# Attention chained into a gated feed-forward layer on one core: the first two batches' softmax, loads and products regrouped, the last output tile cut in two unequal pieces

## The chip, the cores and the metric

The kernel runs on one core of a Trainium2 chip. The time is what the device takes for one execution, in microseconds (us); runs of the same program differ by about 0.1%. Five engines work side by side, each through its own list of instructions in a fixed order: TensorE (PE in the profile; its weight loads have a row of their own, PEld), VectorE (DVE), ScalarE (ACT), GpSimd (POOL) and SyncE (SP). An instruction waits on semaphores, and whatever stands behind it on its engine waits too. Transfers are issued from the lists of POOL, SP and ACT and land later.

## The reference

For 8 batches, 8 heads, 576 tokens and a head size of 64, 32 packed queries per head attend to the keys and values; the tokens then attend to the 32 packed rows. The result, 4608 tokens by 512, goes through a feed-forward layer of 512 by 2048 and 2048 by 512.

```python
def sm_attn(qq, kk, vv):
    s = scale * np.matmul(qq, kk.transpose(0, 1, 3, 2))
    s = s - np.max(s, axis=-1, keepdims=True)
    a = np.exp(s)
    a = a / (np.sum(a, axis=-1, keepdims=True) + 1e-09)
    return np.matmul(a, vv)
p_packed = sm_attn(p, k, v)
out = sm_attn(q, p_packed, p_packed)
...
h = x @ w_in
g = np.where(pos, h, np.where(neg, 0.0, (h + beta) ** 2 / (4.0 * beta)))
return (g @ w_out).astype(np.float32)
```

With beta = 1, pos is h >= 1 and neg is h <= -1.

## The kernel before, in words

All products are in bf16. Each batch goes through these steps, named as in the code.

- **trans** (line 369) turns keys and queries by 12 TensorE transposes per four heads, followed by a copy out of PSUM (`kT`, `qT`). From batch 3 on the transpose is a DMA issued by SP (`turned`, line 511).
- **scores** (387): packed queries times keys, then Exp on ACT (`ex`).
- **packed** (405): `ex` times values, and the sums of `ex` by a matmul with ones (`pk`); the two halves of the tokens are added into `ppT`, and `rs` takes reciprocals of the sums. Batch 0 does this by halves of the heads (g = 0, 1), the other batches at once.
- **weights** (444): for each g, `s2` (tokens' queries times `ppT`), Exp to `eT` on ACT, `sm` (the sums of `eT` by a matmul with blocks of ones), Ln, then Exp of minus that (`rc`) on ACT, and `A` = `eT` times `rs` times `rc` on DVE.
- **mk** (485): `M` = packed rows times `w_in`, in four pieces f of 512 columns, each copied out of PSUM by ACT or DVE. The attention's second product and the layer's first are so folded into one.
- **hidden_tile** (542), 16 per batch: `h` = M times A, four matmuls of 288 columns; on ACT Prelu (`x`, first); second, an add and max on DVE or a Relu on ACT; third, on DVE, min and multiply into `hT`. Tile fi needs piece fi // 4 of M and both g of A.
- **out_tile** (585): per pair of batches nine tiles of 128 tokens, each the sum of 16 steps, matmuls of 512 columns over `hT` and `w_out`. Tiles 0 to 3 of a pair need the first batch alone, tile 4 both. The first pair's tiles 0 to 3 are cut after step 12 (`cuts`): the sum so far is copied to `part` and added at the end. A finished tile is copied to `ob` and stored in rows of 512 floats from SP. The very last tile is computed as two halves of 256 columns, copied by ACT and DVE at once and stored from their two queues (`done_last`).

The order of all this is made when the program is built: every step is a `Task` with a cost per engine from the table `C`, a key and its dependencies, and `Plan.run` (109) puts the tasks, by estimated times, into the engines' lists. A step that may go to either of ACT and DVE (`both`) goes where it is expected to end first. The order on the chip is then fixed; `C` decides order and engine, not durations. PSUM has three double slots (`W`), which all products but the output tiles share, and two slots for output tiles (`O`); five buffers hold `x`. While fewer than three output slots have been taken, the planner fills TensorE's expected waits with matmuls on zeros (`FILL`).

Loads go from POOL's list in the order of the lines 291 to 312: batch 0 in halves of four heads, in the order `FIRST` (k, v, q, k, v, q); then pieces of `w_in` and `w_out` in turns; then batch 1's k (two halves), v (one load), q (two halves), the last piece of `w_out` and the rest of p.

Of the kernel before, what the change touches and what calls it, by code (L numbers as in the profile page):

```python
# [11 lines left out]
C = dict(load=3.5666, half=1.46, w_in=2.57, w_out=2.57, rest=1.25, out=9, p=4.05, land=2.0125, xt=6.5, xland=11, tpp=0.06, tp=0.042, sc=0.034, pk=0.9765, s2=0.2862, sm=0.245, M=0.2415, h=0.49, o=0.217, switch=0.05, join=0.1604, pTc=0.1, Tca=1.12, Tcd=0.76, ex=0.82, ppT=0.42, ppo=0.41, ppa=0.4, ppd=0.2, rs=0.18, eT=0.74, ln=0.65, rc=0.68, A=0.82, Mca=1, Mcd=1.22, x=0.65, ta=0.683, td=0.489, hT=0.758, oba=0.585, obd=0.6276, array=0.2, wake=1.2, warm=4.2, early=0.3, tell=0.034, feed=0.085, slack=0.51, margin=0.1717, wait=0.5)  # L12
NW, NO, NX, NB = 3, 2, 5, 6
DW, FILL = 256, 512
TURNED = 3
# [166 lines left out]
def kernel(  # L182
# [108 lines left out]
    FIRST = [("k", 0), ("v", 0), ("q", 0), ("k", 1), ("v", 1), ("q", 1)]  # L291
# [9 lines left out]
    add_weights("in", 0)  # L301
    add_weights("in", 1)
    add_weights("out", 0)
    add_weights("in", 2)
    add_weights("out", 1)
    add_weights("in", 3)
    add_weights("out", 2)
    add_load("k", 1, 2)
    add_load("v", 1, 1)
    add_load("q", 1, 2)  # L310
    add_weights("out", 3)
# [46 lines left out]
    def attention(b, key):  # L358
# [9 lines left out]
        def trans(nm, i, dst, prev):  # L368
# [11 lines left out]
            t = add(PE, C["tp"] * 12, ky, [L[nm, b, i]] + prev, mm, takes="W", readers=1, mode=0)  # L380

            def cp(eng):
                w = 4 * E * TP
                copy(dst()[:, i, :w].rearrange("p (j c) -> p j c", j=X), box["tp"][:, :, :w // 2])(eng)
            return t, [both(cp, C["Tca"], C["Tcd"], ky, [t], frees=t)]
# [58 lines left out]
        def weights(g, deps, r):  # L444
# [10 lines left out]
            def exp2(eng):  # L455
                box["eT"] = att.tile([P, X, HALF], bf16, tag="eT", name="eT")
                nc.scalar.activation(box["eT"], box["s2"][:, :, :HALF], AF.Exp, scale=rs()[:, g, 1:])  # L457

            def mm2():
                sm = box["sm"] = wide([P, X, FW], f32, "sm")  # L460
                for x in range(X):
                    nc.tensor.matmul(sm[:, x, :HALF], onesblk, box["eT"][:, x], start=True, stop=True)  # L462

            def ln(eng):
                box["ln"] = att.tile([P, X, HALF], f32, tag="ln", name="ln", bufs=1)
                nc.scalar.activation(box["ln"], box["sm"][:, :, :HALF], AF.Ln)  # L466

            def inv(eng):
                box["rc"] = att.tile([P, X, HALF], f32, tag="rc", name="rc")
                nc.scalar.activation(box["rc"], box["ln"], AF.Exp, scale=-1.0)  # L470

            def norm(eng):
                nc.vector.scalar_tensor_tensor(A()[:, g], box["eT"], rs()[:, g, :1], box["rc"], ALU.mult, ALU.mult)  # L473
            p_ = K.get((b - 1, "A" + str(g)), [])
            t, j = yield ky, C["s2"], deps + p_, mm
            e_ = add(ACT, C["eT"], ky, [t, r] + p_, exp2, frees=(t, j))
            t2 = add(PE, C["sm"], km, [e_], mm2, takes="W", readers=1, mode=0)
            l_ = add(ACT, C["ln"], km, [t2] + last.get("ln", []), ln, frees=t2)
            i_ = add(ACT, C["rc"], km, [l_] + p_, inv)
            a_ = add(DVE, C["A"], km, [i_] + K.get((b - 2, "h"), []), norm)  # L480
            last["ln"] = [i_]
            K[b, "A" + str(g)] = [a_]
            yield t, e_, a_

        def mk(f, deps):
# [13 lines left out]
            if (b, f) == (0, 0):  # L499
                yield t, add(DVE, C["Mcd"], ky, [t], cp, frees=(t, j))  # L500
# [206 lines left out]
```

## Time and profile before

| what | us |
|---|---|
| median of 3 runs | 250.54 (250.51 to 250.75) |
| the profiled execution's own time | 249.87 |
| its span, from the first to the last instruction | 247.8 |
| PE busy within the span | 237.5 (96%) |
| DVE busy | 180.7 (73%) |
| ACT busy | 186.2 (75%) |

The profiled execution took 0.67 us less than the median of the runs, and 2.07 us of it lie outside the span. Matmuls are pipelined, so that their busy times overlap; in the rows of the timeline the distance of two starts says more than a duration. In rows of groups the columns are line, engine, operation, tiles, shapes and count, then busy us and mean ns of one, then the engine's idle time before them and who ended it. A window's row has the busy time of PE, PEld, DVE, ACT and POOL, the granted clock of TensorE, the DMA engines' share and GB/s.

### The profile page before, as it was taken

What the parts mean: (1) busy time and instruction counts of PE and PEld (TensorE: products, weight loads), DVE (VectorE), ACT (ScalarE), POOL (GpSimd) and SP (SyncE); (2) the same over time, 40 slices, a digit from 0 to 9 for tenths busy, and PEclk for the clock granted to TensorE, in tenths of its full rate; (3) what the DMA queues carried; (4) which work ended last, traced back from release to release, by engine and by line L of the source; (5) the groups of instructions that cost most, each with busy time, mean ns of one, the idle gap of its engine ahead of it and who ended that gap; (6) DMA issues with size and microseconds to landing.
All of it is one profiled execution on the core that took longest, in us unless ns stands there. A gap on an engine that the chain in (4) does not pass through costs nothing.

```text
span 247.8 us, 5398 instructions
## 1 busy us (share of the span) xinstructions
PE 237.5 (96%) x2191; PEld 137.5 (55%) x2191; DVE 180.7 (73%) x312; ACT 186.2 (75%) x294; POOL 29.3 (12%) x44
## 2 busy tenths in 40 slices
PE   7879899999989999999999999999999999999993
PEld 2545466467636744665456644665466546654452
DVE  5455998889997987798859884799579967992000
ACT  3358895899889998698769888698888886982110
POOL 8632331212001030011001100000000000000000
PEclk9999999999999999999999999999999999999998
DMA  6999999999999999879998984641571121112223
GB/s 100 201 207 207 206 203 196 203 221 257 167 191 154 237 205 222 193 108 171 151 171 141 163 166 93 138 93 38 95 93 42 33 54 44 45 42 85 56 74 85
DMA packets 54825, 34.37 MB, mean 139 GB/s; under 512 B 27536, under 2 KB 50320, under 8 KB 54800
## 3 DMA queue, kind: packets, MB, share of 16 engines
q0 software_dynamic: 24672, 18.55, 50.0%
q1 hardware_dynamic: 29968, 15.34, 31.9%
q8 instruction: 17, 0.28, 0.5%
q10 hardware_dynamic: 160, 0.13, 0.2%
q14 instruction: 8, 0.07, 0.1%
HBM read 37.22 MB, written 9.44 MB: 188 GB/s over the span
## 4 chain that ended last, share of the span: by engine, by line
PE 79%; DMA 10%; DVE 6%; ACT 2%; issue 1%; POOL 1%; ACTq 0%; POOLq 0%
PE o L601 47%; PE h L549 21%; DMA w_in_sb<-in_moe_w_in_dram 8%; PE mp L494 3%; DVE hT L564 3%; DMA k<-in_k_dram 3%; PE pk L418 2%; PE sp L398 2%; PE tp L377 2%; PE sm L462 1%; DVE x L559 1%; PE s L452 1%; PE pk L424 1%; DVE pT L320 1%; ACT rc L470 1%
## 5 line engine op out<-in xcount | busy, mean ns | idle before, releaser
L601 PE MATMUL o<-w_out_sb,hT 128*128 128x512 bf16 (+1 forms) x592 | 144.5, 374 | 0.7 <-DVE hT L564 0.6
L564 DVE SCALAR_TENSOR_TENSOR hT<-x 128x576 bf16<-128x576 f32 x128 | 94.5, 755 | 5.4 <-ACT x L561 2.6
L554 ACT ACTIVATE x<-h 128x576 f32<-128x576 f32 x128 | 77.8, 656 | 12.6 <-PE h L549 9.9
L601 PEld LDWEIGHTS <-hT 128*128 128x128 bf16 x592 | 55.8, 98 | 55.7 <-issue 5.8
L549 PE MATMUL h<-A,M 128*128 128x288 bf16 x512 | 75.1, 286 | 0.5 <-ACT M L320 0.5
L549 PEld LDWEIGHTS <-M 128*128 128x128 bf16 x512 | 49.5, 98 | 21.5 <-issue 1.1
L559 DVE TENSOR_SCALAR x<-x 128x576 f32<-128x576 f32 x87 | 39.9, 458 | 11.0 <-ACT x L554 11.0
L561 ACT ACTIVATE x<-x 128x576 f32<-128x576 f32 x41 | 27.2, 683 | 0.1
L320 ACT COPY ob<-o 128x512 f32<-128x512 f32 (+1 forms) x19 | 10.9, 575 | 19.4 <-PE o L601 19.3
L320 DVE COPY ob<-o 128x512 f32<-128x512 f32 (+1 forms) x14 | 9.4, 668 | 22.0 <-PE o L601 22.0
L320 ACT CAST M<-mp 128x1024 bf16<-128x1024 f32 x22 | 21.3, 1019 | 3.2 <-PE mp L494 3.2
L473 DVE SCALAR_TENSOR_TENSOR A<-eT,rs,rc 128x576 bf16<-128x576 bf16 x16 | 13.0, 814 | 6.1 <-ACT rc L470 6.1
L320 DVE CAST M<-mp 128x1024 bf16<-128x1024 f32 x10 | 12.1, 1220 | 6.4 <-PE mp L494 6.4
L401 ACT ACTIVATE ex<-sp 96x768 bf16<-96x768 f32 x16 | 13.0, 813 | 4.4 <-PE sp L398 4.3
L457 ACT ACTIVATE eT<-s,rs 128x576 bf16<-128x576 f32 x16 | 11.3, 740 | 4.7 <-PE s L452 4.7
L466 ACT ACTIVATE ln<-sm 128x576 f32<-128x576 f32 x16 | 10.4, 651 | 3.8 <-PE sm L462 3.4
L260 POOL DMA_DIRECT2D q<-in_q_dram x10 | 7.4, 744 | 47.6 <-DMA qT<-q 33.3
L494 PE MATMUL mp<-w_in_sb,ppT 64*32 64x512 bf16 x256 | 10.5, 380 | 2.3 <-DMA w_in_sb<-in_moe_w_in_dram 2.2
L260 POOL DMA_DIRECT2D k<-in_k_dram x10 | 7.5, 753 | 44.1 <-DMA kT<-k 27.5
L676 PE MATMUL o<-zeros 128*128 128x512 bf16 (+1 forms) x39 | 10.8, 406 | 1.2 <-DVE zeros L248 1.2
L470 ACT ACTIVATE rc<-ln 128x576 f32<-128x576 f32 x16 | 10.9, 683 | 0.5
L398 PEld LDWEIGHTS <-kT 128*128 128x128 bf16 x192 | 7.6, 98 | 2.8 <-DVE kT L320 1.0
(50 smaller groups left out, 117.2 us busy)
## 6 DMA issues: line engine op xcount, KB each, us to landing
out_dram<-ob SPq DMA_DIRECT2D x23, 192.0 KB, 2.8
v<-in_v_dram POOLq DMA_DIRECT2D x7, 576.0 KB, 18.3
k<-in_k_dram POOLq DMA_DIRECT2D x6, 576.0 KB, 12.4
q<-in_q_dram POOLq DMA_DIRECT2D x6, 576.0 KB, 12.1
out_dram<-ob SPq DMA_DIRECT2D x24, 128.0 KB, 2.9
w_in_sb<-in_moe_w_in_dram POOLq DMA_DIRECT2D x4, 512.0 KB, 14.6
w_out_sb<-in_moe_w_out_dram POOLq DMA_DIRECT2D x4, 512.0 KB, 16.9
out_dram<-ob SPq DMA_DIRECT2D x23, 64.0 KB, 2.0
```

The costliest lines, as they stand in the source:

```text
L260: nc.gpsimd.dma_start(tok[nm, b][:, hs].rearrange("p h c d -> p h (c d)"), SRC[nm][b, hs].rearrange("h (p c) d -> p h (c d)", c=NC))
L320: return lambda eng: nc.vector.tensor_copy(out_, in_) if eng == DVE else nc.scalar.copy(out_, in_)
L401: nc.scalar.activation(ex()[:, :, i].rearrange("p e x a n -> p e (x a n)"), box["sp"], AF.Exp, scale=scale)
L470: nc.scalar.activation(box["rc"], box["ln"], AF.Exp, scale=-1.0)
L473: nc.vector.scalar_tensor_tensor(A()[:, g], box["eT"], rs()[:, g, :1], box["rc"], ALU.mult, ALU.mult)
L494: nc.tensor.matmul(mp[a * NP:(a + 1) * NP, g], pp_of(y, h), w_in_sb[y * D:(y + 1) * D, h // 2, f * FW:(f + 1) * FW], start=True, stop=True)
L549: nc.tensor.matmul(h[:, hf, :HALF], T[b, "M"][:, g, fi * P:(fi + 1) * P], T[b, "A"][:, g, hf], start=(g == 0), stop=(g == G - 1))
L554: nc.scalar.activation(box["x"], box["h"][:, :, :HALF], AF.Prelu, bias=-1.0, alpha=0.5)
L559: nc.vector.tensor_scalar(x, x, 1.0, 0.0, ALU.add, ALU.max)
L561: nc.scalar.activation(x, x, AF.Relu, bias=1.0)
L564: nc.vector.scalar_tensor_tensor(hT[:, fi, col:col + S].rearrange("p (a t) -> p a t", a=2), box["x"], 1.0, box["x"], ALU.min, ALU.mult)
L601: nc.tensor.matmul(o, hT[:, fi, i * P:(i + 1) * P], w_out_sb[:, fi, cs], start=(fi == 0 or fi in cuts), stop=(fi + 1 in cuts))
```

## The change

- The table `C` has new estimates, three new entries (`klo`, `khi`, `part`), and the keys of batch 0 and of the later batches are in another order.
- Loads: batch 0 comes as k0 k1 v0 q0 v1 q1. What follows is `ORDER`: three pieces of `w_in` and two of `w_out`, then batch 1's first half of k, of v and second half of k, the last piece of `w_in`, and so on; batch 1's v comes in halves too, and its `packed` step goes by halves of the heads.
- Batch 0: the copies of turned keys and queries are two instructions each; the softmax of g = 1 (`eT`, `sm`, `ln`, `rc`, `A`) goes by halves of the tokens, 288 columns each; every piece of M waits for the sums `sm` of g = 1; the first piece of M is copied in two halves, by g. M's pieces 1 to 3 wait for hidden tiles 0, 4 and 8.
- The first pair: two tiles instead of four are cut, after 8 steps instead of 12.
- The last batch: `A` is written in another order of the tokens, by two instructions per g, and rows are stored by that order.
- The last tile: two pieces of 384 and 128 columns, one after the other on TensorE; the first is copied by DVE and stored from SP, the second copied and stored by ACT.

```diff
+PARTS, CUT = 2, 8
+ORDER = "i0 i1 i2 o0 o1 k0 v0 k1 i3 v1 o2 q0 q1 o3"
...
-    FIRST = [("k", 0), ("v", 0), ("q", 0), ("k", 1), ("v", 1), ("q", 1)]
+    FIRST = [(nm[0], int(nm[1])) for nm in "k0 k1 v0 q0 v1 q1".split()]
...
+            parts = [slice(j, j + 1) for j in range(X)] if b == 0 else [slice(X)]
...
-            return t, [both(cp, C["Tca"], C["Tcd"], ky, [t], frees=t)]
+            part = 0.55 if len(parts) > 1 else 1.0
+            return t, [both(lambda eng, js=js: cp(eng, js), C["Tca"] * part, C["Tcd"] * part, ky, [t], frees=t) for js in parts]
...
+            parts = [slice(x, x + 1) for x in range(X)] if (b, g) == (0, 1) else [slice(X)]
...
+            def norm(eng, xs):
+                if b == B - 1:
+
+                    for x in range(X):
+                        o, e, r_ = [v.rearrange(w, e=E) for v, w in ((A()[:, g, x], "p (t e) -> p t e"),
+                                    (box["eT"][:, x], "p (e t) -> p t e"), (box["rc"][:, x], "p (e t) -> p t e"))]
+                        nc.vector.scalar_tensor_tensor(o, e, rs()[:, g, :1], r_, ALU.mult, ALU.mult)
+                    return
...
+            first_sm = K[b, "sm1"] if b == 0 else []
+            n = G if (b, f) == (0, 0) else 1
+            t, j = yield ky, C["M"], deps + [L["in", f]] + K.get((b - 2, "h"), []) + first_sm, mm, n
...
-        pk, pc, r = zip(*([packed((0,), [e0]), packed((1,), [e1])] if b == 0 else [packed((0, 1), [e0, e1])] * G))
+        pk, pc, r = zip(*([packed((0,), [e0]), packed((1,), [e1])] if b == 0 or b == 1 and "v0" in ORDER else [packed((0, 1), [e0, e1])] * G))
...
-        cuts = [12, KF] if pr == 0 and i < 4 else [KF]
+        cuts = [CUT, KF] if pr == 0 and i < PARTS else [KF]
+        pieces = [slice(0, 3 * d_model // 4), slice(3 * d_model // 4, d_model)] if end else [slice(0, d_model)]
...
+            elif end:
+                add(ACT if j else DVE, C["oba"] if j else C["obd"], b_key(pr, i), prev, fn,
+                    frees=owner, takes="ob", holds=C["out"])
...
-    names = "kT0 sc0 pk0 qT0 s20 kT1 sc1 pk1 sm0 qT1 s21 M0 sm1 M1 M2 M3".split()
+    names = "sc0 kT0 qT0 kT1 sc1 pk0 s20 pk1 sm0 s21 sm1 M0 M1 qT1 M2 M3".split()
...
+            for f in range(1, NF):
+                K[b, "M"][f].deps.append(K[b, "h"][4 * f - 4])
```

188 lines of the change are left out of this document (106 added, 82 removed).

## The prediction

> **What bounds the kernel now.** On the page TensorE is busy nearly throughout, so I read the busy times by stretch first, and then the timeline of the stretches where it is not full.
>
> ```profile
> 0.00:20.64 20.64, 16.43 (x185) 8.39 (x186) 10.16 (x26) 9.02 (x15) 12.14 (x22) 1.00 1.10 173
> 20.64:49.06 28.42, 27.09 (x300) 16.05 (x298) 24.75 (x41) 23.31 (x37) 7.82 (x10) 1.00 1.33 203
> 49.06:72.95 23.89, 23.09 (x243) 14.55 (x242) 21.92 (x40) 22.92 (x34) 2.32 (x3) 1.00 1.28 210
> 72.95:218.40 145.45, 145.45 (x1333) 85.59 (x1333) 117.81 (x198) 122.63 (x197) 7.01 (x9) 1.00 0.72 123
> 218.40:243.90 25.50, 25.46 (x135) 12.91 (x132) 5.64 (x10) 8.04 (x15) 0.00 (x0) 1.00 0.29 73
> 243.90:247.80 3.90, 0.00 (x0) 0.00 (x0) 0.42 (x1) 0.26 (x1) 0.00 (x0) 0.83 0.23 67
> ```
>
> From 72.95 us on TensorE is busy 145.45 of 145.45 us: nothing is to be won there, only lost. The change can win in three places: the 20.64 us before the first hidden tile (mostly matmuls on zeros and waits), the 1.33 + 0.80 us that TensorE stands idle up to 72.95, where VectorE and ScalarE are busy over 90% of the third stretch, and the 3.9 us after the last matmul.
>
> ```profile
> 1.20 2.96 PE L676 MATMUL o<-zeros 128*128 128x512 bf16 x7 [1.20 <-DVE zeros L248]
> 4.46 2.00 PE L676 MATMUL o<-zeros 128*128 128x512 bf16 x9
> 10.64 0.68 PE L377 MATMUL tp<-ident,k 96*128 96x96 bf16 x12 [0.17 <-DMA k<-in_k_dram]
> 13.54 0.68 PE L377 MATMUL tp<-ident,q 96*128 96x96 bf16 x12 [0.59 <-DMA q<-in_q_dram]
> 15.41 0.49 PE L452 MATMUL s<-qT,ppT 64*32 64x288 bf16 x8
> 17.02 0.41 PE L494 MATMUL mp<-w_in_sb,ppT 64*32 64x512 bf16 x8 [1.12 <-DMA w_in_sb<-in_moe_w_in_dram]
> 17.81 0.41 PE L462 MATMUL sm<-eT,onesblk 128*128 128x288 bf16 x2
> 19.54 0.41 PE L494 MATMUL mp<-w_in_sb,ppT 64*32 64x512 bf16 x8 [0.46 <-DMA w_in_sb<-in_moe_w_in_dram]
> 20.64 3.13 PE L549 MATMUL h<-A,M 128*128 128x288 bf16 x24
> 29.70 0.41 PE L494 MATMUL mp<-w_in_sb,ppT 64*32 64x512 bf16 x8 [0.60 <-DMA w_in_sb<-in_moe_w_in_dram]
> ```
> ```profile
> 14.26 0.76 DVE L320 COPY qT<-tp 128x1152 bf16<-128x1152 bf16 x1 [2.14 <-PE tp L377]
> 17.51 1.22 DVE L320 CAST M<-mp 128x1024 bf16<-128x1024 f32 x1 [1.05 <-PE mp L494]
> 18.31 0.65 ACT L466 ACTIVATE ln<-sm 128x576 f32<-128x576 f32 x1 [1.60 <-PE sm L462]
> 19.00 0.68 ACT L470 ACTIVATE rc<-ln 128x576 f32<-128x576 f32 x1
> 19.71 0.82 DVE L473 SCALAR_TENSOR_TENSOR A<-eT,rs,rc 128x576 bf16<-128x576 bf16 x1 [0.98 <-ACT rc L470]
> 21.33 3.91 ACT L554 ACTIVATE x<-h 128x576 f32<-128x576 f32 x7 [0.31 <-PE h L549]
> ```
>
> Read the chain to 20.64: the last q half lands at 13.5; transposes, copy, s at 15.41; then the sums sm stand in TensorE's list behind M's first piece, which waits for its weights until 17.02, so sm starts at 17.81 though ScalarE had long ended eT; ln, rc and A follow, and A ends at 20.53. Landings are paced: a half of 288 KB per (13.54 - 10.64) / 2 = 1.45 us, a piece of weights per (29.70 - 19.54) / 4 = 2.54 us (four lie between those waits).
>
> **The change, part by part**, by the order that the changed planner writes.
>
> *Head.* Loads: the six halves end at 13.5 as before; the first weights at 17.0 and 19.5; then by 2.54 and 1.45: third w_in 22.1, w_out 24.6 and 27.2, batch 1's k 28.6, v 30.1, k 31.5, the last w_in 34.1 (29.7 before), v 35.5, w_out 38.1, q 39.5 and 41.0. Copy of q in two halves, both on VectorE: ends about 15.1, as before. Sums now stand ahead of M: eT by halves 15.5 to 16.4, sm 16.0 and 16.4, then ln, ln, rc, rc. A half costs by two ScalarE copies below (512 columns 0.586, 256 columns 0.372) the same fixed 0.16 and half the rest, so 0.41 and 0.44 for ln and rc: rc ends 17.45 and 17.8. VectorE's half of M's copy, 17.5 to 18.15, stands ahead of the two A: these end at 18.6 and 19.05. ScalarE's half of M is ready at 18.45. TensorE has M at 17.02, then seven zeros matmuls (0.216 each, as an output step below) until 18.87: hidden tile 0 starts at 18.9, all 1.7 us earlier, of which M's second piece, now behind it, takes back 0.34.
>
> [...]
>
> *18.9 to 49: new waits.*
>
> ```profile
> L564 DVE SCALAR_TENSOR_TENSOR hT<-x 128x576 bf16<-128x576 f32 x128 | 94.5, 755 | 5.4 <-ACT x L561 2.6
> L559 DVE TENSOR_SCALAR x<-x 128x576 f32<-128x576 f32 x87 | 39.9, 458 | 11.0 <-ACT x L554 11.0
> L561 ACT ACTIVATE x<-x 128x576 f32<-128x576 f32 x41 | 27.2, 683 | 0.1
> L320 ACT CAST M<-mp 128x1024 bf16<-128x1024 f32 x22 | 21.3, 1019 | 3.2 <-PE mp L494 3.2
> L320 ACT COPY ob<-o 128x512 f32<-128x512 f32 x18 | 10.5, 586 | 16.6 <-PE o L601 16.5
> L320 DVE COPY ob<-o 128x512 f32<-128x512 f32 x13 | 8.9, 687 | 3.2 <-PE o L601 3.2
> L320 DVE COPY kT<-tp 128x1152 bf16<-128x1152 bf16 x2 | 1.5, 758 | 1.3 <-PE tp L377 1.3
> L320 DVE COPY pT<-tpp 64x768 bf16<-64x768 bf16 x3 | 1.6, 549 | 0.9 <-ACT pT L320 0.9
> 218.56 25.31 PE o L601 x133
> 156.36 1.96 PE h L549 x16
> ```
>
> A hidden tile takes TensorE 0.49 us (1.96 / 4), an output step 0.216 (25.31 over 101 steps and 32 of half width). M's second piece follows hidden tiles 0 to 2, and its copy (1.02, ScalarE) stands behind three x and one Relu: x starts 0.69 after its tile (20.64 to 21.33) and the next 0.56 later, so x at 19.6, 20.1, 20.6, Relu 21.3 to 22.0, copy until 22.85. Tile 4 needs it: TensorE, done with tile 3 at 21.2, fills 5.5 zeros matmuls and goes on at 22.95: 1.75 lost (0.55 less if the copy were never late, 1.0 more if it slipped by one copy). Tiles 4 to 7 and M's third piece then run to 25.4, eight output steps to 27.15, just when the second w_out lands (27.2); tile 8; then batch 1's keys, due at 28.6, hold TensorE for 0.55 (up to 1.45 more if the transfers are one half later, nothing if earlier). From there I find some 0.15 us of small waits up to the end of M: each later load (31.5, 34.1, 35.5, 38.1, 39.5, 41.0) lands before TensorE asks for it, and the last four hidden tiles follow M's last piece from about 37. Lost in all 2.45, against 1.33 idle before (and shorter waits, which overlapping busy times hide).
>
> Batch 1's hidden tiles then start at 50.7 rather than 49.06, but TensorE has by then done five output steps (1.08) and two sets of key transposes of batch 2 (1.04) that came later before: as if at 48.6, ahead by 0.45. By the single terms it is 1.7 - 0.34 - 2.45 + 1.33 = 0.24 and the waits that the busy times hide.
>
> *50 to 73.*
>
> ```profile
> 49.06 0.65 PE L549 MATMUL h<-A,M 128*128 128x288 bf16 x4 [0.47 <-ACT M L320]
> 72.73 0.39 PE L601 MATMUL o<-w_out_sb,hT 128*128 128x512 bf16 x1 [0.56 <-DVE hT L564]
> 64.48 0.76 DVE L564 SCALAR_TENSOR_TENSOR hT<-x 128x576 bf16<-128x576 f32 x1
> 65.65 0.76 DVE L564 SCALAR_TENSOR_TENSOR hT<-x 128x576 bf16<-128x576 f32 x1
> ```
>
> Before, this stretch ends on VectorE, at 1.17 us per tile (64.48 to 65.65). Between batch 1's last A and its last hT VectorE's list loses one part copy and one addition (0.69 each), one add-and-max (0.46), two pT copies (1.1) and the copy of p (0.43), and gains a copy each of kT and qT (0.76 each): 1.85 less. I walk its last hT to 70.8 instead of 72.67, and TensorE through tiles 4 and 5 with 0.3 us of waits, instead of 0.80 idle and some shorter ones: finished at 71.45 instead of 72.95. Both then stand at the same place, M's pieces of batch 2: ahead by 1.5 us.
>
> *73 to 218.* Matmuls the same. M's pieces 1 to 3 move behind the softmax sums, and the sums stand 14 or more output steps (3.0 us) ahead of the first hidden tile, which ln, rc and A (0.65 + 0.68 + 0.82) fit into. In the last batch A as four strided halves (0.5 each, perhaps 0.3 more) lies beside 22 output steps and three pieces of M. Cost: 0; below nothing is impossible, since TensorE is full, and above see the rivals.
>
> *Tail.*
>
> ```profile
> 243.78 0.37 ACT L320 COPY ob<-o 128x256 f32<-128x256 f32 x1 [2.80 <-PE o L601]
> 243.89 0.42 DVE L320 COPY ob<-o 128x256 f32<-128x256 f32 x1 [18.80 <-PE o L601]
> 244.34 0.79 SPq L622 DMA_DIRECT2D out_dram<-ob  x2
> DMA to landing us min/median/max: 1.9/2.1/2.4
> ```
>
> Matmul columns are the same. Before: DVE's copy to 244.31, two transfers issued one after the other, the second 0.37 later, landed 2.1 later at 246.8; the span ends 1.0 after. Now 128 columns are left when the matmuls end: a ScalarE copy of 0.27 (the step from 512 to 256 columns carried on) from 243.89, one transfer at 244.2, landed 246.1 to 246.3. The 384 columns are copied 0.9 earlier (0.56) and land by 246.0. Won 0.6 (0.4 to 0.7).
>
> *Sum:* 1.5 + 0.6 = 2.1; I take 2.0, since a walk leaves out small waits. The profiled execution took 249.87 with a span of 247.8; so span 245.8, execution 247.9, and against the median, which stands 0.67 higher, 250.54 - 2.0 = 248.5.
>
> **The rivals.**
>
> 1. *The early start runs dry.* If M's second copy or batch 1's keys come later by the upper ends above, or the last w_in, 4.4 us later than before, holds tiles 12 to 15 and with them VectorE, the 1.5 is eaten and the tail stays: 250.54 - 0.6 = 249.9. For it speaks that every load and every VectorE gap counts here; against it that output tiles 2 and 3 give TensorE work in between, and that VectorE's list is shorter.
> 2. *Slower: the clock.* The rows at 1.20 and 4.46 show zeros matmuls at 0.42 and then at 0.22 each: TensorE runs at half rate until some 3 us of dense matmuls have passed. The change issues 5.5 instead of 6.5 of them first and only 1.5 before 7 us, none between p's transposes (4.5) and the keys (6.3). If half rate stays, the filler before tile 0 lasts twice 1.51 and M another 0.34, 1.85 later, and hidden tiles for some 3 us at half rate lose 1.5 more: 248.5 + 3.35 = 251.9. It decides for slower once more than 2 us are lost so.
> 3. *Slower: a wait per batch in the full stretch*, as the 0.47 at 49.06, because M's pieces now come just ahead of the hidden tiles: 6 x 0.47 = 2.8, so 251.3. With 0.33 each nothing is left of the gain (250.5).
>
> [...]
>
> **How the numbers follow.** My walk: 0.60, with its own range 247.5 to 249.4 (the bounds of the waits). Rival 1: 0.18, 249.4 to 250.4, half of it below 250.0. Rival 2: 0.08; rival 3: 0.10, a third of it within 0.5 of no change. More gained than walked: 0.04. About 0.2% (0.5 us) is what a measurement can tell. Faster 0.60 + 0.04 + 0.09 = 0.73; same 0.09 + 0.03 = 0.12; slower 0.15. The range 247.4 to 250.8 leaves the slower cases out.
>
> **What would show it.** The first hidden tile at 18.9, its sums sm at 16 to 16.6, before M's first piece at 17.0; TensorE waiting before hidden tile 4 on ScalarE's M and before batch 1's keys on the DMA; tiles 4 and 5 done near 71.5; the last landing some 0.6 earlier after the last matmul. Wrong it would be by zeros matmuls at 0.42 after 5 us, by hidden tiles held past 51 us, or by idle TensorE after 73.

## The result, and the profile after

The changed kernel takes 250.69 us (median of 22 runs, 249.89 to 252.03), the kernel before, measured beside it, 250.06 (22 runs, 249.72 to 251.28: runs of one program differ by 0.6% here, not by the 0.1% of the first three). The ratio is 1.0032, 95% interval 1.002 to 1.0045: slower by 0.6 us, near the upper end of the range (250.8) and on the other side of no change, where I had forecast 2.0 less. The changed kernel's times fall into two groups, 15 runs from 249.89 to 250.84 and 7 from 251.59 to 252.03; the profiled run (252.03, span 250.22) is of the second. The kernel before's profiled run took 249.87, 0.19 below its median.

The stretches of the changed kernel, cut at the same events as before: the first hidden tile, batch 1's first hidden tile, the end of output tile 5, the last matmul. The columns are length, then busy time (and instructions) of PE, PEld, DVE, ACT and POOL, the granted clock, DMA share and GB/s.

```profile
0.00:21.68 21.68, 17.00 (x159) 10.12 (x162) 9.31 (x30) 10.48 (x19) 11.95 (x22) 1.00 1.10 173
21.68:54.05 32.37, 30.41 (x337) 18.56 (x342) 27.14 (x46) 27.09 (x42) 9.56 (x12) 1.00 1.33 203
54.05:75.40 21.35, 20.46 (x212) 13.14 (x214) 19.10 (x34) 20.47 (x33) 1.55 (x2) 1.00 1.28 210
75.40:246.90 171.50, 169.22 (x1440) 97.75 (x1464) 124.38 (x206) 130.05 (x212) 7.09 (x9) 1.00 0.74 113
246.90:250.22 3.32, 0.04 (x1) 0.00 (x0) 0.00 (x0) 0.27 (x1) 0.00 (x0) 0.97 0.24 79
```

In the fourth row TensorE was not idle for the 2.28 us that the row leaves: 24 matmuls have no record there (1440, against 1464 weight loads). In e1 of the experiments, which differs by nine matmuls on zeros at the start and has all records there, it is busy 171.35 of 171.45 us.

Five output steps and two sets of key transposes (2.12 us of TensorE) stand ahead of batch 1's first hidden tile now and behind it before, as the prediction says; the table sets them off. It gives for each stretch its length minus that of the kernel before, in us. The last column is the kernel e8 of the experiments, the changed kernel with its clock, its copies and its last store mended.

| stretch | predicted | after | e8 |
|---|---|---|---|
| to the first hidden tile | -1.74 | +1.04 | -1.00 |
| to batch 1's first hidden tile | +1.26 | +1.83 | +1.65 |
| to the end of tile 5 | -1.02 | -0.42 | -0.45 |
| to the last matmul | 0 | +0.55 | +0.50 |
| to the end | -0.60 | -0.58 | -0.59 |
| sum | -2.10 | +2.42 | +0.11 |

(For example, second row, after: 32.37 - 2.12 - 28.42 = 1.83.) The tail came as predicted. The rest did not.

The table sets single traces side by side, and the kernel before's is one of its shorter executions. By it e8 comes out 0.11 longer, while by medians e8 is 0.56 shorter than the kernel before. How far traces of one program differ, e3 and e15 show (both are the kernel before with the new tail alone): their second stretch takes 28.42 and 29.18 us. M's last weights land at 29.62 and 30.36, and only in the second does TensorE wait for them long. First e3, then e15:

```profile
29.66 0.41 PE L501 MATMUL mp<-w_in_sb,ppT 64*32 64x512 bf16 x8 [0.38 <-ACT x L561]
```
```profile
30.41 0.41 PE L501 MATMUL mp<-w_in_sb,ppT 64*32 64x512 bf16 x8 [1.39 <-DMA w_in_sb<-in_moe_w_in_dram]
```

Their last matmuls start at 243.65 and 244.31. A difference below some 0.7 us between the ends of two traces therefore shows nothing by itself; which wait stands where is read from them all the same.

The head, from the timeline of the changed kernel:

```profile
1.19 2.53 PE L728 MATMUL o<-zeros 128*128 128x512 bf16 x6 [1.19 <-DVE zeros L256]
6.87 0.84 PE L728 MATMUL o<-zeros 128*128 128x512 bf16 x2
...
12.61 0.46 DVE L326 COPY qT<-tp 128x576 bf16<-128x576 bf16 x1 [0.76 <-PE tp L383]
...
13.10 0.64 ACT L326 COPY qT<-tp 128x576 bf16<-128x576 bf16 x1 [0.65 <-DVE qT L326]
...
15.49 1.16 PE L383 MATMUL tp<-ident,q 96*128 96x96 bf16 x12
...
16.45 1.48 PE L728 MATMUL o<-zeros 128*128 128x512 bf16 x3
...
18.82 0.28 PE L477 MATMUL sm<-eT,onesblk 128*128 128x288 bf16 x1 [0.20 <-ACT eT L471]
...
19.61 0.28 PE L477 MATMUL sm<-eT,onesblk 128*128 128x288 bf16 x1 [0.50 <-ACT ln L482]
19.82 0.41 PE L529 MATMUL mp<-w_in_sb,ppT 64*32 64x512 bf16 x8
...
20.16 1.69 PE L728 MATMUL o<-zeros 128*128 128x512 bf16 x7
...
21.68 1.63 PE L589 MATMUL h<-A,M 128*128 128x288 bf16 x12
```

Three things are to be seen. Matmuls on zeros start 0.42 us apart up to those at 16.45 and 0.22 from 20.16 on, and twelve transposes take 1.16 instead of 0.68: TensorE runs at half rate until 17.94, where the granted clock is first recorded (before: 4.14). The second half of a copy, on ScalarE, starts when VectorE's first half ends, and names it as what it waited for. And the second half of the sums waits for the Ln of the first. The sums do stand ahead of M's first piece, as predicted, but at 18.82 and 19.61 instead of 16.0 and 16.4.

Around batch 1's first hidden tile, and the tail:

```profile
51.02 1.59 ACT L326 COPY pT<-tpp 64x768 bf16<-64x768 bf16 x2
...
52.64 0.56 DVE L326 COPY pT<-tpp 64x768 bf16<-64x768 bf16 x1 [1.14 <-ACT pT L326]
53.23 0.76 DVE L326 COPY kT<-tp 128x1152 bf16<-128x1152 bf16 x1
53.24 0.79 ACT L326 COPY pT<-tpp 64x768 bf16<-64x768 bf16 x1 [0.63 <-DVE pT L326]
...
54.05 1.83 PE L589 MATMUL h<-A,M 128*128 128x288 bf16 x12 [0.93 <-DVE kT L326]
...
246.14 0.56 DVE L326 COPY ob<-o 128x384 f32<-128x384 f32 x1 [24.71 <-PE o L647]
...
247.02 0.27 ACT L326 COPY ob<-o 128x128 f32<-128x128 f32 x1 [2.91 <-PE o L647]
247.31 0.37 ACTq L662 DMA_DIRECT2D out_dram<-ob  x1
```

The pT copies of batches 2 to 7 alternate between ScalarE and VectorE, one after the other, and with them VectorE's copy of kT, which holds the slot that the hidden tile waits for. My walk had no wait there. The row gives it as 0.93; counted from where the last output step would have let TensorE go on (nine of them, 0.216 apart, from 51.01) it is 1.09, since a matmul's recorded time reaches some 0.16 beyond the start of the next. Waits of TensorE below are counted in this second way unless a row is named. The last copy takes the 0.27 forecast.

### The profile page after: what moved, and what is told of

The parts are those of the page before. It is cut to its first block, busy times and chain, and to the rows that moved or that the text cites. A ratio compares the mean times of both kernels' runs of the same rounds, so it can differ in the third digit from the quotient of the medians.

```text
span 250.2 us, 5377 instructions
## 1 busy us (share of the span) xinstructions
PE 237.1 (95%) x2145; PEld 139.6 (56%) x2181; DVE 179.9 (72%) x313; ACT 188.4 (75%) x306; POOL 30.1 (12%) x45
## 4 chain that ended last, share of the span: by engine, by line
PE 80%; DVE 8%; ACT 7%; issue 2%; DMA 2%; ACTq 0%; POOLq 0%
PE o L647 43%; PE h L589 22%; DVE hT L604 5%; PE mp L529 3%; PE sp L407 3%; PE tp L383 3%; ACT x L594 2%; PE pk L427 2%; DVE x L599 2%; DMA k<-in_k_dram 2%; PE sm L477 1%; PE o L728 1%; PE s L461 1%; ACT x L601 1%; DVE kT L326 1%
## 5 line engine op out<-in xcount | busy, mean ns | idle before, releaser
L647 PE MATMUL o<-w_out_sb,hT 128*128 128x512 bf16 (+2 forms) x558 | 134.7, 373 | 2.7 <-issue 1.6
L326 ACT COPY ob<-o 128x512 f32<-128x512 f32 (+1 forms) x26 | 14.9, 572 | 28.3 <-PE o L647 27.3
L601 ACT ACTIVATE x<-x 128x576 f32<-128x576 f32 x46 | 30.9, 681 | 0.3
L326 DVE COPY ob<-o 128x512 f32<-128x512 f32 (+1 forms) x9 | 6.0, 672 | 26.0 <-PE o L647 25.3
L326 DVE CAST M<-mp 128x1024 bf16<-128x1024 f32 (+1 forms) x15 | 17.7, 1184 | 4.9 <-PE mp L529 4.8
L326 ACT CAST M<-mp 128x1024 bf16<-128x1024 f32 (+1 forms) x18 | 17.5, 989 | 3.0 <-PE mp L529 3.0
L471 ACT ACTIVATE eT<-s,rs 128x576 bf16<-128x576 f32 (+1 forms) x17 | 11.5, 712 | 3.5 <-PE s L461 3.5
L497 DVE SCALAR_TENSOR_TENSOR A<-eT,rs,rc 128x576 bf16<-128x576 bf16 (+1 forms) x15 | 11.5, 774 | 2.2 <-ACT rc L487 2.0
L482 ACT ACTIVATE ln<-sm 128x576 f32<-128x576 f32 (+1 forms) x17 | 10.6, 624 | 1.4 <-PE sm L477 1.1
L487 ACT ACTIVATE rc<-ln 128x576 f32<-128x576 f32 (+1 forms) x17 | 11.0, 654 | 0.4
## 6 DMA issues: line engine op xcount, KB each, us to landing
v<-in_v_dram POOLq DMA_DIRECT2D x6, 576.0 KB, 14.9
```

Of the source, the lines that this page charges most:

```text
L326: return lambda eng: nc.vector.tensor_copy(out_, in_) if eng == DVE else nc.scalar.copy(out_, in_)
L601: nc.scalar.activation(x, x, AF.Relu, bias=1.0)
L647: nc.tensor.matmul(box["o", j][:, :cs.stop - cs.start], hT[:, fi, i * P:(i + 1) * P], w_out_sb[:, fi, cs], start=(fi == 0 or fi in cuts), ...
```

## Experiments

Times are medians; a ratio is to the kernel before on the same chip, with its 95% interval. "h0" is the start of the first hidden tile; "the last hT" is batch 1's, behind which tiles 4 and 5 end. Theories and rivals are those that stand above each result.

**e1: the clock.** The changed kernel with nine more matmuls on zeros.

```diff
+            if cast: zero_mms(1)   # ahead of p's transposes
...
+            if cast: zero_mms(8)   # behind them
```

> The changed kernel with nine more matmuls of 512 columns on zeros: one ahead of p's transposes, eight behind them; all else in the same order. If the late clock is the cause: full rate granted by 4.2 to 7.7 us instead of 17.94, the first hidden tile at about 19 us instead of 21.68, tiles 4 and 5 finished near 71.5 instead of 75.4, time about 2 us below the kernel before (248.1 beside its 250.1) and no second group of slower runs. If the new order itself is what costs: the clock comes early too, but the time stays within 0.5 us of the changed kernel's 250.7.

250.32 us (12 runs), ratio 1.0011 (0.9996 to 1.0027). The clock is granted at 5.30 and h0 moves from 21.68 to 20.28; the span falls from 250.22 to 248.58. So the late clock is worth 1.64 us between these two profiled runs, of which the changed kernel's is one of its slower group, and about 0.4 between medians. With the clock early the kernel is still no faster than the one before: the second expectation holds, the new order itself costs, and the 2 us of the first did not come. Two groups remain: eight runs at 249.76 to 250.38 and four at 251.17 to 251.37, these with a mean granted clock of 0.993 against 0.998 to 1.000. That mean takes in the time behind the last matmul (0.83 in the last stretch of the kernel before), so it does not tell where the clock was low, and the cause of these four stays open.

**e2: the same loss in the kernel before?** It without one of its first 6.5 matmuls on zeros and without the next 8.5.

```diff
+        if len(calls) == 6 or 8 <= len(calls) <= 16:
+            return
```

> The kernel before without 1 of the 6.5 zeros matmuls ahead of p's transposes and without the 8.5 behind them; nothing else changed. If the late clock is the cause of the changed kernel's loss: the clock is granted only after 7 us, in some runs near 18 us, and the time rises by 1 to 3 us over 250.1 with runs in two groups. If not: within 0.3 us of the kernel before, since those matmuls compute nothing.

250.23, ratio 0.9994 (0.9981 to 1.0007). The clock came 5.85 us later (9.99 instead of 4.14) and by the medians cost nothing: TensorE waits for M's first weights either way, until 17.02 before and until 16.47 here. So in this kernel a clock that comes by 10 us costs nothing, since it does not reach the chain to h0.

**e3: the tail alone.** The kernel before with the changed kernel's last tile and last batch's A.

> The kernel before with the changed kernel's ending alone: last batch's tokens in the other order, the last tile as 384 and 128 columns one after the other. By the prediction's tail term 0.4 to 0.7 us faster (0.6), with the last landing that much nearer to the last matmul. If the strided A of the last batch or the single large transfers cost as much: no change within 0.2 us.

249.44, ratio 0.9971 (0.9959 to 0.9982): 0.7 us faster than the kernel before. The tail term holds.

**e4: whole copies.** The kernel of e1, with batch 0's copies of keys and queries whole on VectorE; all other lists are the same.

```diff
+                if len(parts) > 1:
+                    if js.start: return
+                    js = slice(X)
```

> The kernel of e1_warm, with the same lists on every engine but for one thing: batch 0's four copies of turned keys and queries are whole again (768 or 0.76 us each on VectorE, none on ScalarE). Theory 1 (the two halves of a copy that went to two engines ran one after the other, VectorE 0.46 and then ScalarE 0.64, so halving made the chain longer): the scores of the first keys and s of g = 0 end some 0.35 us earlier, the first hidden tile moves from 20.28 to about 19.9 to 20.1, execution 0 to 0.4 us below e1. Theory 2 (halves help, as the change supposes): the first hidden tile is later, 20.5 to 20.7, and the time 0.2 to 0.4 above e1. Theory 3 (the head is not what decides, later loads are): no difference at tiles 4 and 5, time within 0.15 of e1.

251.74, ratio 1.0069 (1.0046 to 1.0093): a longer time, yet h0 is at 19.64 (e1: 20.28), tile 5 ends 0.65 earlier and the last matmul starts at 244.41 instead of 245.06. Of the 0.64, the first q half landed 0.28 earlier in this run, which leaves 0.36: theory 1. The rows of the first q copy say the same, 1.13 us from start to end in e1 (two rows) and 0.76 in e4:

```profile
12.37 0.46 DVE L326 COPY qT<-tp 128x576 bf16<-128x576 bf16 x1 [0.65 <-PE tp L391]
12.86 0.64 ACT L326 COPY qT<-tp 128x576 bf16<-128x576 bf16 x1 [0.83 <-DVE qT L326]
```
```profile
12.09 0.76 DVE L326 COPY qT<-tp 128x1152 bf16<-128x1152 bf16 x1 [0.44 <-PE tp L391]
```

What is gained at h0 arrives at the last matmul in full. The time went elsewhere, into the last store. First e4, then e1:

```profile
244.99 0.27 ACT L326 COPY ob<-o 128x128 f32<-128x128 f32 x1 [3.19 <-PE o L659]
245.28 2.16 ACTq L674 DMA_DIRECT2D out_dram<-ob  x1
```
```profile
245.36 0.27 ACT L326 COPY ob<-o 128x128 f32<-128x128 f32 x1 [2.91 <-PE o L655]
245.66 0.38 ACTq L670 DMA_DIRECT2D out_dram<-ob  x1
```

**e5: a whole softmax.** The kernel of e1 with eT, sums, ln, rc and A of g = 1 whole, at the second halves' places.

> The kernel of e1_warm with the same lists, but batch 0's softmax of g = 1 in whole instructions, at the places of the second halves. Theory 1 (the halves cost: the second sums wait 0.50 for the Ln of the first, and each extra instruction pays its fixed part): from s at 16.18 the whole chain takes eT 0.74, sums 0.25, ln 0.65, rc 0.68, A 0.82 and the steps between them, so A ends at about 20.2 and the first hidden tile starts at 20.0 to 20.2 instead of 20.28; time 0 to 0.3 below e1. Theory 2 (halves win what the prediction gave them, some 0.5): first hidden tile at 20.7 to 20.9, time up to 0.5 above e1.

252.58 (4 runs), ratio 1.0111 (1.0081 to 1.0142), with the same slow last store (2.40). From the end of s to the point where hidden tiles run without a wait it takes 3.37 us (16.68 to 20.05), in e1 3.46 (16.82 to 20.28). (h0 is at 19.72 in e5, but the tile's third matmul waits for A until 20.29; two matmuls back from there is 20.05.) Whole is as fast as halved: the halves win nothing, as theory 1 has it.

**e6: the old load order for batch 0** in the kernel of e1, planned anew.

```diff
-    ... "k0 k1 v0 q0 v1 q1".split()
+    ... "k0 v0 q0 k1 v1 q1".split()
```

> The kernel of e1_warm with batch 0's halves loaded in the order of the kernel before (k, v, q, k, v, q); the planner makes the lists anew. Theory 1 (keys first costs: the first half of q comes one or two transfers later, 11.6 instead of 9.5, and with it the sums of g = 0, which stand ahead of the second q's transposes in TensorE's list and hold them until 14.9): the second q's transposes start when it lands, 13.5 to 14.0, the first hidden tile at 19.0 to 19.5, and tiles 4 and 5 are done 0.5 to 1 us earlier than in e1 (73.8). Theory 2 (the head does not pass its gain on, since M's second copy or batch 1's keys take it back): first hidden tile earlier, tiles 4 and 5 done within 0.3 of e1.

253.58 (4 runs), ratio 1.0159 (1.0117 to 1.0201), again with a slow last store (the last landing 4.3 after the last matmul, in e1 2.3); the last matmul itself starts 0.97 later than in e1. The second q half lands at 13.36 and its transposes start at 13.91, right behind the sums of g = 0 and 1.0 earlier than in e1, but h0 is at 20.52: the planner gave the second half of that copy to ScalarE, behind rc and a ppT copy, so it ran at 16.08 to 16.72 though VectorE's half began at 14.62. Keys first does hold the second q back; here the halved copy took the gain back. The planner's new order changes more than that, so the time of e6 as a whole says little about the loads.

**e7: sums ahead of M in the kernel of e3.**

```diff
+            first_sm = K[b, "sm1"] if b == 0 else []
```

> The kernel of e3_tail (the kernel before with the changed kernel's tail; 249.44) with one more thing: all pieces of batch 0's M wait for the sums of g = 1, so that the sums stand ahead of M's first piece in TensorE's list. Loads, whole copies and whole softmax are those of the kernel before. Prediction's view: the sums start at about 16.4 instead of 17.8, the first hidden tile at 19.2 to 19.5 instead of 20.6, and the time falls by 0.5 to 1.2 below e3. Rival (the early start runs dry): the first hidden tile is earlier all the same, but TensorE stands before M's later pieces and batch 1's keys for as long, tiles 4 and 5 are done within 0.3 of 72.95, and the time is within 0.2 of e3.

249.56, ratio 0.9974 (0.9961 to 0.9988), no different from e3. The sums start at 17.16 instead of 18.29 and A ends 1.08 earlier (19.93 instead of 21.01), but h0 is at 21.18: M's second piece, whose weights land at 19.8, and five matmuls on zeros stand ahead of it.

**e8: the slow store.** The kernel of e4 with four one-element copies more at the start of ScalarE's list.

```diff
+        for _ in range(4):
+            nc.scalar.copy(tiny_sb[:1, :1], zeros[:1, :1])
```

> The kernel of e4_whole_copies with four ScalarE copies of one element more, at the very start, where ScalarE has nothing to do. In e4 the first hidden tile, tiles 4 and 5 and the last matmul all came 0.65 us earlier than in e1, but the last store from ScalarE's queue took 2.16 us to issue instead of 0.38, while a transfer of the instruction queue stands at 245.93, 0.65 after that issue began; in e1 the same transfer stands at 242.88, while ScalarE waits. Theory (ScalarE's list is fetched in blocks, and in e4 a block's end falls on the last store): with the list four longer the block's end moves back to a wait, the issue takes 0.4 again, and the time is 251.74 - 2.0 = 249.7, some 0.6 below e1. Rival (the slow issue has another cause, such as the store's own queue): the issue stays at 2 us and the time at 251.5 to 251.9.

249.66 (249.10 to 250.08), ratio 0.9976 (0.9965 to 0.9987): 2.1 us less than e4, by four copies that compute nothing. h0 and the last matmul are where they were (19.64, 244.41), and the last store takes 0.38 to issue. The DMA view has one transfer of the instruction queue between 245.9 and 246.3 in e4, during that issue (first fence), and in e1 between 242.8 and 243.5, while ScalarE waits (second); in e8 there is none after 244.4.

```profile
q14 instruction: 1, 0.01, 4.8%
```
```profile
q14 instruction: 1, 0.01, 4.8%
```

ScalarE's lists of e4, e5, e6 and e9, all with the slow store, have 452 or 453 records in the trace; those of the kernels without it 438 to 446 and 454 to 462. The DMA view of the whole span has nine transfers of this queue in e1 and in the changed kernel (0.07 MB in all, so some 8 KB each), eight in the kernel before. That they bring ScalarE's list in blocks, and that the store waits for one of them, no trace shows directly; it is inferred from this transfer's time, from these lengths, and from e8, where four more entries took the wait away as expected. The slow issue took 1.7 to 2.0 us more than the 0.38 (and in e4 and e9 ScalarE's copy ahead of it started 0.28 later).

**e9: the old keys for batches 2 to 7** in the kernel of e8.

> The kernel of e8_tail_moved with the keys of batches 2 to 7 as in the kernel before (order and ends of each batch's interval); batches 0 and 1 keep the new ones. Theory (the 0.6 us that the changed kernel loses between 73 and 243 us, in small waits of hidden tiles on ScalarE's x and on ppT in batches 2 and 7, come from the new order, which packs the hidden tiles closer): these waits go, and the time falls by 0.5 to 0.7 against e8. Rival (they come from the new costs, or from the halves of the last batch's A): within 0.2 of e8.

252.11 (4 runs), ratio 1.0071 (1.0043 to 1.0099). It has the slow store again (2.12), and nothing shows that it would be faster without: the last matmul starts 0.47 later than in e8, which two traces do not tell apart. Putting the old keys back did not bring back the 0.5 us lost between tile 5 and the last matmul.

**e10: all pT copies of batches 2 to 7 on ScalarE** in the kernel of e8.

> The kernel of e8_tail_moved, with the one of the four pT copies of batches 2 to 7 that VectorE made given to ScalarE (all else in its place). Theory (copies into one tile by two engines run one after the other: VectorE's pT waits 1.15 for ScalarE's, and VectorE's copy of kT behind it holds the slot that batch 1's first hidden tile waits for, 0.93): VectorE's kT copy starts some 1.2 earlier, that wait goes or falls below 0.3, batch 1's hidden tiles start 0.6 to 0.9 earlier, and tiles 4 and 5 end 0.3 to 0.9 earlier. Rival (VectorE's list is full up to tile 5 anyway and sets its time): the hidden tiles start earlier, but tiles 4 and 5 end within 0.2 of e8, and the time is the same.

249.95, ratio 0.9981 (0.9971 to 0.9991), no different from e8 within the intervals. Batch 1's first hidden tile no longer waits, the second and third do (0.83 on pT, 0.66 on kT). Tile 5 ends 0.6 later, but the loads landed 0.4 later in this run, so neither theory nor rival is told apart by that. The wait moved. With h0 at 19.17 this run also shows TensorE waiting for batch 1's keys (0.54 and 0.37), as the prediction had it.

**e11: e7, with M's pieces 1 to 3 behind hidden tiles 0, 4 and 8.**

```diff
+                K[b, "M"][f].deps.append(K[b, "h"][4 * f - 4])
```

> The kernel of e7_sums_first (before's loads, whole copies and softmax, the changed tail, sums ahead of M) with one more line of the change: M's pieces 1 to 3 wait for hidden tiles 0, 4 and 8. In e7 A ended 0.75 us earlier than in the kernel before, yet the first hidden tile came at 21.18, since M's second piece (weights at 19.8) and five matmuls on zeros stood ahead of it. Theory (the early start is worth its size when nothing stands ahead of it): first hidden tile at 19.5 to 20.2, tiles 4 and 5 done 0.3 to 0.8 earlier than in e7, time 0.3 to 0.8 below e7's 249.56. Rival (M's copy, now behind three x on ScalarE, stops hidden tile 4 for as long): tiles 4 and 5 within 0.2 of e7's, same time.

250.22, ratio 1.0004 (0.9988 to 1.002), 0.66 above e7. h0 is at 19.65, 1.5 earlier than in e7, but the last hT only 0.33, and even that is not gained: M's last weights landed at 29.52 here and at 30.24 in e7. The early start is given back at three places:

```profile
23.75 1.65 PE L558 MATMUL h<-A,M 128*128 128x288 bf16 x12 [0.81 <-ACT M L321]
...
32.01 0.59 PE L616 MATMUL o<-w_out_sb,hT 128*128 128x512 bf16 x2 [0.47 <-DMA w_out_sb<-in_moe_w_out_dram]
33.53 0.64 PE L378 MATMUL tp<-ident,k 96*128 96x96 bf16 x11 [0.93 <-DMA k<-in_k_dram]
```

With the loads of the kernel before, the early start runs dry, on M's copy, on `w_out` and on batch 1's keys: the mechanism of the prediction's first rival.

**e12: p's transposes for batches 2 to 7 at key 0.75 instead of 0.9** in the kernel of e8 (with eight one-element copies in place of four, as in e13, e14 and e16).

> The kernel of e8_tail_moved with one key changed: the transposes of p for batches 2 to 7 at 0.75 instead of 0.9 (and eight, not four, one-element copies on ScalarE at the start, so that a block's end of its list stays off the last store). The planner then puts only one of batch 2's two key transposes ahead of batch 1's first hidden tiles, so that two of the three W slots, not three, hang on copies of ScalarE and VectorE. In e8 the first hidden tile of batch 1 waits 1.05 us for such a slot. Theory (that wait is worth its size, since TensorE is full from there on): it goes or falls below 0.4, tiles 4 and 5 and the last matmul come 0.5 to 1.0 earlier, time 248.7 to 249.2. Rival (VectorE's list from batch 1's A to its last hT sets the end of tiles 4 and 5 in any case): they end within 0.2 of e8's 73.1, the 0.61 wait for hT there grows by what was won, and the time is within 0.2 of e8's 249.66.

250.90, ratio 1.004 (1.0022 to 1.0058). Batch 1's hidden tiles start 1.34 earlier, but the new order put two A and a copy of M into VectorE's list ahead of the last hT, which ends 2.4 later. It decides neither for the theory nor for its rival.

**e13: the old estimates from batch 2's attention on** in the kernel of e8.

> The kernel of e8_tail_moved with the planner's old estimates of each step's duration (35 entries of the table) for everything from batch 2's attention on, the new ones before; the keys stay new (eight one-element copies at the start as in e12). Theory (the 0.6 us of small waits between 73 and 243 come from the new estimates, after e9 showed that the keys are not the cause): between tile 5's end and the last matmul TensorE takes 170.6 us, as in the kernel before, instead of 171.3, and the time falls by 0.4 to 0.7 against e8. Rival (neither keys nor estimates, but the order of the work at the border of batches 1 and 2): 171.1 or more, time within 0.2 of e8.

250.70, ratio 1.0023 (1.0008 to 1.0039), 1.0 above e8. Putting the old estimates back does not bring the time back either. Like e9 and e12 it makes another order of everything behind it, so it does not clear the estimates of the 0.5 us.

**e14: one of batch 2's key transposes behind batch 1's hidden tile 0**, and **e15: e3 again**, beside it.

```diff
+                K[2, "kt"][1].deps.append(K[1, "h"][0])
```

> The kernel of e8_tail_moved with one dependency more: the second key transposes of batch 2 wait for batch 1's hidden tile 0 (and eight one-element copies at the start). Ahead of batch 1's first hidden tile then stand one set of key transposes and five output steps instead of two and nine; VectorE's list from batch 1's last A to its last hT stays nearly the same (one add and max less, one copy of p and, in place of the first additions, the same two), which e12's did not: there two A and a copy of M came into it. Theory (the 1.05 us wait for a slot is a loss, since it leaves VectorE idle for 3.4 us there against 2.0 in the kernel before): batch 1's hidden tiles start near 50.0 to 50.5, VectorE's idle time falls to about 2.2, its last hT ends at 71.4 to 71.9 instead of 72.64, and the time is 248.7 to 249.1. Rival (the last hT is set elsewhere, by batch 2's attention on ScalarE, 21.3 of 23.4 us busy there): the last hT ends within 0.3 of 72.64, time within 0.2 of 249.66.

> The kernel of e3_tail once more, beside e14 on the same chip, since the two are the candidates for the shortest time. If e14's theory holds, e14 is 0.3 to 0.7 shorter than this one, which should again be 0.25 to 0.35% below the kernel before; if its rival holds, this one is 0.1 to 0.3 shorter.

e14 takes 249.95, ratio 0.999 (0.9976 to 1.0004). Batch 1's first hidden tile starts at 49.61, and the second waits 1.13 for VectorE's kT, which stands behind the pT copies as before. Neither the theory's time (248.7 to 249.1) nor the rival's place of the last hT (72.34 to 72.94) came: it ends at 73.16, VectorE having been idle for 3.86 us. e15 takes 249.16, ratio 0.9964 (0.9951 to 0.9977): the kernel before with the new tail is the fastest of all I ran.

**e16: p's transposes behind batch 1's hidden tile 4** in the kernel of e8.

> The kernel of e8_tail_moved with one dependency more: the transposes of p for batches 2 to 7 wait for batch 1's hidden tile 4 (and eight one-element copies at the start). e10, e12 and e14 moved single copies or transposes, and each time a hidden tile of batch 1 still waited 0.8 to 1.3 us, in e14 behind VectorE's pT copy, which waits 1.14 for ScalarE's. Here none of the four pT copies stands ahead of batch 1's hidden tiles 0 to 3 on any engine. Theory (these copies, one after the other on two engines, hold the slots and ScalarE's x): the first hidden tile starts near 50.0, none of the first four waits over 0.4, VectorE's idle time between A and the last hT falls from 3.4 to below 2.5, its last hT ends at 71.6 to 72.3 instead of 72.64, time 249.0 to 249.4. Rival (what is not waited for here is waited for at batch 2's first scores, which need pT): the last hT within 0.2 of 72.64 or later, time 249.5 or more.

250.74, ratio 1.0025 (1.0011 to 1.0039). Half of the theory holds: the first hidden tile starts at 49.63 and the first four run without a wait. But VectorE is idle later on (0.50, 0.84 and 1.73 us between 54.7 and 60.5, ahead of a pT copy, of an hT that waits for ScalarE, and of a qT copy), and its last hT ends 0.9 later than in e8, as the rival has it. In all four orders of this border VectorE is idle between batch 1's last A and the last hT for longer than the 3.42 us of e8: 4.17 (e10), 3.60 (e12), 3.86 (e14) and 4.91 (e16). Which order would be free stays open.

## Why the prediction was wrong, point by point

The 2.0 us were 0.6 in the tail and 1.5 ahead of it, and the 1.5 is what failed. The first hidden tile was to start at 18.9 and started at 21.68. Of these 2.8 us the late clock took 1.40 in the profiled runs (e1: 20.28), halved copies 0.36 and an early landing 0.28 (e4: 19.64), and the 0.74 that remain are M's first piece, which e4 has at 17.77 instead of 17.02: it stands behind the second sums now, and these come at 17.56 instead of 16.4, since the last q half landed at 14.22 instead of 13.5 and since they wait 0.50 for the first Ln. Behind it came a wait of 1.09 at batch 1's first hidden tile and 0.5 us in the stretch that I had taken as full. The points, in the order of the prediction:

- **"first the clock": rival 2 held, in part.** Its condition came true: half rate stayed until 17.94. Its price was 3.35, measured 1.64 in the profiled runs and 0.4 between medians. Neither term of that price was paid: the filler ahead of tile 0 ran at full rate (seven in 1.69 us from 20.16), and so did the hidden tiles; the 1.40 at h0 was lost ahead of them, in transposes, sums and zeros at half rate. I gave it 0.08, an estimate: I had not asked when the clock would first be granted, which was at 4.14 in the kernel before and at 17.94 here. The stretches of the changed kernel, of a length that I chose:

```profile
7.40:10.80 3.40, 3.02 (x45) 2.58 (x44) 0.96 (x3) 1.45 (x2) 2.28 (x4) 1.00 1.28 191
10.80:14.20 3.40, 2.96 (x42) 1.99 (x39) 1.01 (x5) 1.71 (x3) 1.35 (x2) 1.00 1.28 203
14.20:17.60 3.40, 3.40 (x38) 2.36 (x35) 1.56 (x6) 2.37 (x4) 0.81 (x2) 1.00 1.24 208
```

  The grant did not come behind the two with 3.02 and 2.96 us busy; it came 0.34 us behind the end of the third, which has no idle time. But the busy time of such a stretch does not tell the grant, and the prediction's "some 3 us of dense matmuls" is what the kernel before shows, no rule. Below are 3.41 us of the changed kernel, with five and a half zeros and no grant at their end, and the 3.41 us ahead of the grant in the kernel before (4.14, six and a half zeros) and in e13 (3.90), both with less busy time than the 3.02 and 2.96 above:

```profile
0.87:4.28 3.41, 2.53 (x6) 0.73 (x6) 2.79 (x12) 1.15 (x1) 2.90 (x6) 1.00 0.54 78
```
```profile
0.73:4.14 3.41, 2.94 (x7) 0.89 (x7) 2.65 (x12) 1.28 (x1) 2.76 (x6) 1.00 0.50 70
```
```profile
0.49:3.90 3.41, 2.71 (x7) 0.89 (x7) 2.45 (x7) 2.83 (x9) 2.54 (x5) 1.00 0.43 64
```

  So the grant came behind 2.71 us of matmuls on zeros in one run, and not behind 2.53 in another nor behind 3.02 of mostly shorter matmuls and transposes. That the one zeros matmul dropped at the start made the clock late in this run is inferred from that; no run takes that one alone out or puts it alone back, and e1, with the grant at 5.30, puts nine in. In the kernels that start with six and a half zeros or more the grant came between 3.90 (e13) and 7.04 (e7). Whether the two groups of times go back to the time of the grant is not shown, since the grants of the other runs are not on record.

- **"Copy of q in two halves, both on VectorE: ends about 15.1, as before"** failed. Two of the four copies went to both engines and ran one after the other: 0.36 at h0 (e4). For the second q, both halves were on VectorE as I said, but its transposes started at 14.9 (e1), not 13.5: with keys first the first q lands one or two transfers later, and its sums, 0.40 on TensorE, stand ahead of them in the list. I had taken landings of six halves as a whole and not asked which comes when.
- **"rc ends 17.45 and 17.8"**, by halves of 0.41 and 0.44: the sizes are right (0.16 and half of the rest is 0.42 for the second; 0.41 and 0.43 measured), the gain is not there, since the second sums wait 0.50 for the first Ln (e5: whole is as fast).
- **M's second copy, "1.75 lost before hidden tile 4"**, holds: in the changed kernel tile 3's matmuls end at about 24.1 and tile 4 starts at 25.78. The wait for batch 1's keys did not come since all was later; it came when h0 was early (e10, e11).
- **"From there I find some 0.15 us of small waits"** failed by the wait at batch 1's first hidden tile, 1.09 in the changed kernel and 1.05 in e8 (0.93 and 0.89 in the rows).
- **VectorE's list, "1.85 less"**: between batch 1's last A and its last hT it is busy 19.93 us instead of 21.74, 1.81 less. But it is idle for 3.42 instead of 1.97, at the pT copies and until the first x arrives. I had counted work and taken the idle time as it was.
- **"Cost: 0" from 73 on**: 0.50 to 0.55 us, in waits of hidden tiles for ScalarE's x and for ppT in batches 2, 6 and 7, of 0.1 to 0.2 each. Rival 3 had the place, not the size. Neither the old keys (e9) nor the old estimates (e13) alone brought it back; the cause stays open.
- **Tail, -0.6**: holds (0.58; e3 and e15 0.7 to 0.9 by ratio).

With clock, copies and last store mended (e8, ratio 0.9976) the kernel is 0.6 us faster than before, no more than its tail alone gives (e3 0.9971, e15 0.9964). So all that the change does ahead of the tail gains nothing that can be measured. The early start is handed on when nothing stands in its way (e4: 0.64 at h0, 0.65 at the last matmul), but the change spends it on M's second copy, on batch 1's first hidden tile and in the full stretch.

## What to carry to other kernels

Before halving a step so that two engines share it, look in the profile for a wait between two copies into one tile: if they are named as waiting for each other, halves on two engines can cost more than the whole (here 1.13 us against 0.76). A list made by a planner shifts as a whole: of five edits of a line or two (e10, e11, e12, e14, e16) each moved the wait that it was made for, and none made the kernel faster: two left the time as it was (e10, e14), three cost 0.7 to 1.2 us. So count idle time of the second engine, not only its work. Compare last matmul, last store and end apart, or a slow store passes for a slow kernel. And take two traces of one program before reading tenths from one: here they lie 0.7 us apart.

## What the runs showed of the hardware that I had not expected

- The clock stayed at half until 17.94 us in the changed kernel with TensorE 87 to 89% busy from 7.40 to 14.20, though in the kernel before the grant came at 4.14 behind 3.41 us that were 86% busy, with longer matmuls. The windows' clock column says 1.00 there, and the trace's clock record begins with the grant (17.94); the distance of two matmuls tells (0.42 against 0.22). The stretch at full rate lasts 232.11 us there and 242.35 in the kernel before.
- ScalarE's last store took 2.12 to 2.40 us to issue in four kernels (e4, e5, e6, e9) instead of 0.38 in e1 and e8; in e4 a transfer of the instruction queue stands within that issue. One record less in a list of 454 (e1 to e4) turned a gain of 0.65 at the last matmul into a loss of 1.4.
- The same loads land up to 1.1 us apart from run to run (the last q half at 13.36 in e5, 14.50 in e1), which is more than most steps of this change. In e3 and e15, one kernel, M's last weights land 0.74 apart, and the last matmul starts 0.66 apart.
